# A first layer by seven products: second products added in the accumulator, and one more pair's sums moved

## The chip, the cores and the metric

The kernel runs on one core of a Trainium2 chip. A core has five engines with queues of their own: TensorE (PE; its weight loads are shown as PEld), VectorE (DVE), ScalarE (ACT), GpSimd (POOL) and SyncE (SP), which here only starts transfers. TensorE writes its products into eight accumulator banks of 128 x 512 fp32 values; ScalarE and VectorE read them there. Engines wait for each other through semaphores, and each runs its own instructions in the order in which they were written. The metric is the device time of one execution in microseconds, as the median of several runs.

## The reference

One transformer block with adaptive layer norms on 2048 rows of 512 values: a linear attention block with 32 heads, then a dense layer of 1792 columns with Mish and a dense layer back. The change lies in the second half:

```python
def _B_ref(x, w1, b1, w2):
    h = jnp.einsum("bsd,df->bsf", x, w1) + b1
    sp = jnp.log1p(jnp.exp(-jnp.abs(h))) + jnp.where(h > 0, h, jnp.zeros_like(h))
    act = h * jnp.tanh(sp)
    return jnp.einsum("bsf,fd->bsd", act, w2)

x = x + ga * _A_ref(h, A_wqkv, A_wo)
h = _layernorm(x, axis=-1) * (1 + cb) + sb
x = x + gb * _B_ref(h, B_w1, B_b1, B_w2)
```

## The kernel before

Every product of two fp32 matrices is made from three TensorE products of rounded halves: each operand is split into a high part (a ScalarE copy) and a low part (a VectorE subtraction), and hi*hi, hi*lo and lo*hi are summed in one bank (`mm3`, lines 65 to 69; `split`, 71 to 81).

The rows are worked on in four blocks of 512. The two dense layers take the blocks two at a time, with a scheme of seven products in place of eight (Strassen's, in Winograd's form) for a 2 x 2 arrangement. In the first layer the arrangement is two blocks by one *pair* g of 128-column groups of w1 (f = 2g and 2g + 1, seven pairs). `pair_unit` makes one pair's four results, each 128 x 512, from products named after their left operand:

- c11 = a11*b11 + a12*b21
- u2 = a11*b11 + s2*t2; u3 = u2 + s3*t3
- c12 = u2 + s1*t1 + s4*b22; c22 = u3 + s1*t1; the fourth is u3 + a22*t4

One `product` is six 512-column matmuls into one bank. `add` (917) is a VectorE addition of a bank and an SBUF tile. u1 is the ScalarE copy of a11*b11 out of its bank. Results go through ScalarE's Mish: `mish` (884) also splits the result at once, for the block that goes on first; `mish_b` (906) only keeps it (`ub`), for the other block.

Banks come in three kinds (`PBUFS`, 36): four "acc", three "h", one "tp". A product asks for one of a kind, and gets one that is free, or will be.

The order of work is written out by hand. Side work (splits, sums of w1's rows in `rows`, scaling and splitting w2 in `w2_job`, the layer norm of later tiles in `norm_tile`) are generators: `spawn` enters one, and each `tick` moves all of them on by one step, which puts its instructions behind those written before on their engines. An engine waits at its first unready instruction.

The stages from 200 us on: (1) the a11 and a12 products of pairs 0 and 1, between the last products of the attention output (`o_unit`); (2) for blocks 0 and 1, seven passes of `pair_unit`, each followed by the second layer of block 0 for the pair before (`trail`, `d_unit`, into the four "acc" banks `oacc`); (3) the second layer of block 1 (`second`); (4) for blocks 2 and 3 (the last block pair, L = 2), seven passes over `pairs = [5, 6, 0, 1, 2, 3, 4]`, with the second layer's first two of seven sums, m1 and m2 (`e_unit` for the pass before, four half-width "acc" banks, 24 matmuls of 256 columns, first met in pass n = 1); (5) the tail: the second layer's other sums m4, m6, m7, m5, m3, seven units each.

The tail needs *left sums* of the kept results: `left_sums` makes for one pair a split and four VectorE sums, `left_trail` runs it beside the passes of stage 4 for the first four pairs, and in the tail `ahead_of` (1145) holds what is left to prepare, one item per unit, a few units ahead of its use: the left sums of the last three pairs, then the splits for m6, m7, m5 and m3.

In the profile's names p_a and p_s are banks of products whose left operand begins with a or s, m those of the second layer's sums, l_ the left factors' halves (l_m_5l is the low half for m6 of pair 5), and buffer numbers are left out.

Of the kernel before, what the change touches and what calls it, by code (L numbers as in the profile page):

```python
# [10 lines left out]
AF = mybir.ActivationFunctionType  # L11
# [14 lines left out]
def block_kernel(ctx: ExitStack, tc: tile.TileContext, x, wqkv, wo, w1, b1t, w2, c, wmodt, out):  # L26
    nc = tc.nc
    act, dve, pool, pe, sp = nc.scalar, nc.vector, nc.gpsimd, nc.tensor, nc.sync
# [9 lines left out]
    def sb(name, dt=F32, shape=(P, 512)):  # L38

        return big.tile(list(shape), dt, tag="T", name=name, bufs=SLOTS)  # L40

    def ps(tag, name, shape=(P, 512)):
        return psp.tile(list(shape), F32, tag=tag, name=name, bufs=PBUFS[tag])
# [6 lines left out]
    def spawn(gen):  # L50
        fresh.append(gen)

    def tick():

        running.extend(fresh)
        fresh.clear()
        for g in list(running):
            if next(g, "end") == "end":
                running.remove(g)
# [5 lines left out]
    def mm3(o, st, mv, start, stop):  # L65

        pe.matmul(o, st[0], mv[0], start=start, stop=False)  # L67
        pe.matmul(o, st[0], mv[1], start=False, stop=False)  # L68
        pe.matmul(o, st[1], mv[0], start=False, stop=stop)  # L69

    def split(name, t, keep, key, lo_engine=dve, hi_engine=act):

        hi, lo = sb(f"{name}h", F32R, t.shape), sb(f"{name}l", F32R, t.shape)
        if hi_engine is act:
            act.activation(hi, t, AF.Copy)
        else:
            hi_engine.tensor_copy(hi, t)
        if lo_engine is dve:
            yield
        lo_engine.tensor_tensor(lo, t, f32(hi), op=ALU.subtract)  # L80
        keep[key] = hi, lo
# [18 lines left out]
    c0 = sb("c0")  # L100
# [71 lines left out]
    mv, rs, nb = {}, {}, {}  # L172
# [324 lines left out]
    w2s, w2d, w2f, op_a = {}, {}, {}, {}  # L497
# [9 lines left out]
    def w2_job(f, wait=2):  # L507
        if f not in w2r:
            load_w2(f)
            for _ in range(wait):  # L510
                yield
        t = w2r[f]
        dve.tensor_tensor(t, t, bc["gb"], op=ALU.mult)
        yield
        yield from split(f"w2_{f}", t, w2s, f)
        yield
        g, n = f // 2, f % 2
        if n == 0:
            w2f[g] = drp.tile([P, 2, D], F32, name=f"w2f_{g}")
            for i in range(2):  # L520
                w2d[g, i] = drp.tile([P, 2, D], F32R, name=f"w2d_{g}_{i}")
        for i in range(2):
            pool.dma_start(w2d[g, i][:, n, :], w2s[f][i])
        if g < KEPT:
            pool.dma_start(w2f[g][:, n, :], t)
# [49 lines left out]
    def rows(g, wait):  # L575

        r = [sb(f"w1p_{g}_{i}", F32, (P, 4, P)) for i in range(2)]
        for i in range(2):
            f = 2 * g + i
            sp.dma_start(r[i], w1[:, P * f:P * (f + 1)].rearrange("(k p) f -> p k f", p=P))  # L580
        for _ in range(wait):
            yield
        a11, a12, a21, a22 = [r[i][:, 2 * k:2 * k + 2, :] for i in range(2) for k in range(2)]
        s12, s34 = [sb(f"s{n}_{g}", F32, (P, 4, P)) for n in (12, 34)]
        s1, s2, s3, s4 = s12[:, 0:2, :], s12[:, 2:4, :], s34[:, 0:2, :], s34[:, 2:4, :]
        dve.tensor_tensor(s1, a21, a22, op=ALU.add)
        dve.tensor_tensor(s2, s1, a11, op=ALU.subtract)
        dve.tensor_tensor(s3, a11, a21, op=ALU.subtract)
        dve.tensor_tensor(s4, a12, s2, op=ALU.subtract)
        yield  # L590
        keep, todo = {}, []
        op_rows[g] = keep
        for name, v, parts in (("a1", r[0], ("a11", "a12")), ("s12", s12, ("s1", "s2")), ("s34", s34, ("s3", "s4")),
                               ("a22", a22, ("a22",))):
            half = split(f"{name}_{g}", v, keep, name)
            next(half)
            todo.append((name, half, parts))
            if len(todo) == 2:
                yield
                for name, half, parts in todo:  # L600
                    run(half)
                    for i, part in enumerate(parts):
                        op_a[g, part] = [h[:, 2 * i:2 * i + 2, :] for h in keep[name]]
                todo = []
# [3 lines left out]
    def store_rows(g):  # L608
        for name, halves in op_rows.pop(g).items():
            for i, h in enumerate(halves):  # L610
                rows_d[g, name, i] = drp.tile(list(h.shape), F32, name=f"rd_{g}_{name}_{i}")
                sp.dma_start(rows_d[g, name, i], f32(h))
# [151 lines left out]
    def load_back(key, src, b, t):  # L764
        v = xt[key, b, t] = sb(f"{key}b_{b}_{t}")
        sp.dma_start(v, src.pop((b, t)))

    hf, op_b = {}, {}
# [89 lines left out]
    for b in range(1, NB):  # L858
        for t in range(4):
            n = 4 * b + t  # L860
# [23 lines left out]
    def mish(p, b, f):  # L884
        u = ua[f] = sb(f"u_{b}_{f}")
        act.activation(u, p, AF.Mish, bias=b1c[:, f:f + 1])  # L886
        yield from split(f"a_{b}_{f}", u, ag, (b, f))
# [18 lines left out]
    def mish_b(p, f):  # L906

        u = ub[f] = sb(f"ub_{f}")
        act.activation(u, p, AF.Mish, bias=b1c[:, f:f + 1])  # L909

    def product(g, left, right, tag="h"):
        p = ps(tag, f"p_{left}_{g}")
        for c in range(2):
            mm3(p, [h[:, c, :] for h in op_a[g, left]], op_b[right, c], c == 0, c == 1)
        return p

    def add(out, p, u):
        dve.tensor_tensor(out, p, u, op=ALU.add)  # L918

    def pair_first(c0, g):  # L920

        u1, c11 = sb(f"u1_{g}"), sb(f"c11_{g}")
        act.activation(u1, product(g, "a11", "b11"), AF.Copy)
        add(c11, product(g, "a12", "b21"), u1)
        spawn(mish(c11, c0, 2 * g))
        return u1

    def pair_unit(c0, g, u1=None):

        f = 2 * g  # L930
        whole = u1 is None
        u2, u3, c12, c22 = [sb(f"{n}_{g}") for n in ("u2", "u3", "c12", "c22")]
        if whole:
            u1 = sb(f"u1_{g}")
            act.activation(u1, product(g, "a11", "b11"), AF.Copy)  # L935
        add(u2, product(g, "s2", "t2"), u1)
        add(u3, product(g, "s3", "t3", "tp"), u2)
        tick()
        p = product(g, "s1", "t1")
        add(c12, p, u2)  # L940
        add(c22, p, u3)
        mish_b(c22, f + 1)
        add(c12, product(g, "s4", "b22"), c12)
        mish_b(c12, f)
        tick()
        add(u3, product(g, "a22", "t4", "tp"), u3)
        spawn(mish(u3, c0, f + 1))
        if whole:
            add(u1, product(g, "a12", "b21"), u1)
            spawn(mish(u1, c0, f))  # L950
        tick()

    def prep_a(b, f):
# [35 lines left out]
            load_wb(6)  # L989


    begun = {}
    for g in range(2):
        begun[g] = pair_first(0, g)
        tick()
    for t in (2, 3):
        o_unit(NB - 1, t, "h")
# [2 lines left out]
    def trail(f):  # L1000
        if tiles:
            spawn(tiles.pop(0))
        d_unit(0, f, f)
        ahead(1, f)
        tick()

    for g in range(G + 1):
        if g < G:
            for f in (2 * g, 2 * g + 1) if g else ():
                spawn(w2_job(f))  # L1010
            if g == 0:
                spawn(rows(2, 3))
            pair_unit(0, g, begun.pop(g, None))
            if g < G - 2:
                store_rows(g)
            if 0 < g < G - 2:
                spawn(rows(g + 2, 2))
            if g == G - 1:
                for n in range(8):
                    load_back("n", nd, 2 + n // 4, n % 4)  # L1020
        for f in ((0,), (1,))[g] if g < 2 else (2 * g - 2, 2 * g - 1):
            trail(f)
# [2 lines left out]


    L = NB - 2
    pairs = [5, 6, 0, 1, 2, 3, 4]
    banks, rq, U = {}, {}, {}

    def load_r(n, c):
# [38 lines left out]
    left, sums_of = {}, {}  # L1070

    def left_trail(g):
        yield
        yield
        yield from left_sums(g)
# [48 lines left out]
    for n, g in enumerate(pairs):  # L1124
        if n < 5:
            if n:
                load_rows(n)
            if n:
                load_wb(pairs[n + 1])
        if n == 5:  # L1130
            load_wb(pairs[6])
            load_r(0, 0)
        if n == 6:
            for m in pairs[:5]:
                load_wt("m4", m)
        pair_unit(L, g)
        if n < 4:
            spawn(left_trail(g))
        if n:
            e_unit(n - 1)  # L1140
            tick()

    names = ["m4", "m6", "m7", "m5", "m3"]
    units = [(name, n) for name in names for n in range(G)]
    ahead_of = units[4:]
    loads = list(units)
    loads = loads[5:]
    load_r(1, 0)
# [22 lines left out]
    for t in range(4):  # L1171
        p = last[t][:, 0:D // 2]
# [38 lines left out]
```

## Time and profile before

| | us |
|---|---|
| median of 3 runs | 499.28 (499.13 to 499.49) |
| the profiled execution's own time | 499.34 |
| its span on the chip | 497.6 |

The span runs from the first to the last instruction of the program; some 1.7 us lie around it. A row of the timeline gives start, duration, engine, line, operation and tiles; several like instructions in a row are merged (x2), and in brackets stands how long the engine had been idle and what ended that. TensorE's matmuls overlap: the next one starts before one has ended, so their pace is read from start to start. The profile's busy shares, its waits and its timeline are shown where the prediction uses them.

### The profile page before, as it was taken

To read this page: it belongs to the slowest core of one execution; us is meant where nothing else is said; L and a number is where in the kernel's file an instruction comes from. 1 tells how busy PE (TensorE), PEld (TensorE's weight loads), DVE (VectorE), ACT (ScalarE), POOL (GpSimd) and SP (SyncE) were. 2 spreads that over 40 slices of the span, in tenths; PEclk is the share of its full clock that TensorE was granted. 3 is DMA by queue.
4 is the path that set the end of the run, shared out by engine and by line. 5 is a ranking of instruction groups with operands and counts; after the bars stand their busy time and mean duration, and the time that the engine had idled before them with its cause. 6 is when DMAs were issued, how large, how long until landed. Compare 5 with 4: busy or idle time off the path is not lost.

```text
span 497.6 us, 7730 instructions
## 1 busy us (share of the span) xinstructions
PE 490.2 (98%) x2648; PEld 412.9 (83%) x2648; DVE 394.6 (79%) x758; ACT 265.2 (53%) x472; POOL 136.8 (27%) x238
## 2 busy tenths in 40 slices
PE   7999999999999999999999999999999999999997
PEld 6778888878778888888888888888888888899997
DVE  6889775889997979986977786689878777489771
ACT  6776674533351979727677775187244444366300
POOL 3471000100212323100343333324564221544200
PEclk9999999999999999999999999999999999999999
DMA  8821413381454307298899686999998263878312
GB/s 298 295 84 44 157 33 107 129 275 43 142 139 129 96 30 251 92 366 270 239 344 312 227 278 201 335 321 383 377 343 221 66 173 86 218 189 243 91 43 86
DMA packets 65614, 96.49 MB, mean 194 GB/s; under 512 B 7277, under 2 KB 31733, under 8 KB 65574
## 3 DMA queue, kind: packets, MB, share of 16 engines
q1 hardware_dynamic: 37220, 52.51, 31.7%
q0 software_dynamic: 28208, 43.21, 30.7%
q8 instruction: 21, 0.34, 0.3%
q10 hardware_dynamic: 146, 0.26, 0.2%
q14 instruction: 19, 0.16, 0.1%
HBM read 62.92 MB, written 33.03 MB: 193 GB/s over the span
## 4 chain that ended last, share of the span: by engine, by line
PE 79%; issue 11%; POOL 4%; DVE 3%; DMA 1%; ACT 1%; POOLq 0%; DVEq 0%; ACTq 0%
PE oacc L69 5%; PE oacc L68 5%; PE oacc L67 5%; PE p_s L69 3%; PE p_s L68 3%; PE p_s L67 3%; PE o L67 3%; PE pq L67 3%; PE o L69 3%; PE o L68 3%; PE pq L69 3%; PE pq L68 3%; PE m L69 3%; PE m L68 3%; PE m L67 3%
## 5 line engine op out<-in xcount | busy, mean ns | idle before, releaser
L909 ACT ACTIVATE ub<-c,b1c 128x512 f32<-128x512 f32 x28 | 19.5, 720 | 57.3 <-DVE c L918 45.3
L918 DVE TENSOR_TENSOR u<-p_s,u 128x512 f32<-128x512 f32 x28 | 19.4, 692 | 22.8 <-PE p_s L69 12.0
L189 POOL TENSOR_TENSOR rs_n<-rs_n,half 128x1 f32<-128x1 f32 x16 | 9.8, 613 | 52.2 <-DVE rs_n L215 42.4
L918 DVE TENSOR_TENSOR u<-p_a,u 128x512 f32<-128x512 f32 x26 | 17.4, 687 | 8.3 <-PE p_a L69 8.3
L918 DVE TENSOR_TENSOR c<-p_s,u 128x512 f32<-128x512 f32 x28 | 18.0, 684 | 4.6 <-PE p_s L69 4.6
L1122 POOL DMA_DIRECT2D wt_m<-w2t x20 | 14.0, 702 | 23.3 <-PE p_s L69 15.1
L775 ACT ACTIVATE hf_n<-tp_n,mc 128x512 f32<-128x512 f32 x16 | 11.7, 772 | 16.2 <-PE tp_n L773 16.2
L886 ACT ACTIVATE u<-u,b1c 128x512 f32<-128x512 f32 x26 | 18.6, 715 | 2.8 <-DVE u L918 2.5
L241 ACT ACTIVATE e_q<-pq 128x512 f32<-128x512 f32 x16 | 9.4, 588 | 19.9 <-PE pq L69 19.9
L241 ACT ACTIVATE e_k<-pk 128x512 f32<-128x512 f32 x16 | 9.3, 590 | 13.2 <-PE pk L69 12.9
L189 POOL TENSOR_TENSOR rs_x<-rs_x,half 128x1 f32<-128x1 f32 (+1 forms) x10 | 7.1, 717 | 32.8 <-DVE rs_x L184 32.0
L573 POOL DMA_DIRECT2D w2b<-w2d x20 | 10.7, 538 | 18.4 <-DMA out_dram<-r 5.3
L243 DVE TENSOR_SCALAR e_k<-e_k 128x512 f32<-128x512 f32 x16 | 6.8, 426 | 10.1 <-ACT e_k L241 9.9
L681 POOL DMA_DIRECT2D rden_d<-rden x3 | 2.2, 740 | 43.8 <-DVE rden L679 43.8
L198 ACT ACTIVATE x<-x,nb_x,rs_x 128x512 f32<-128x512 f32 x15 | 11.6, 808 | 4.6 <-DVE nb_x L193 3.5
L567 POOL DMA_DIRECT2D wb<-w2d x14 | 9.9, 710 | 13.1 <-PE p_a L69 9.6
L935 ACT ACTIVATE u<-p_a 128x512 f32<-128x512 f32 x12 | 7.1, 588 | 10.8 <-PE p_a L69 10.1
L693 DVE TENSOR_TENSOR q<-q,rd 128x512 f32<-128x512 f32 x16 | 10.5, 686 | 2.3 <-DMA rd<-rden_d 2.2
L198 ACT ACTIVATE r<-r,nb_n,rs_n 128x512 f32<-128x512 f32 x8 | 6.5, 809 | 10.1 <-DVE nb_n L219 9.2
L705 DVE TENSOR_TENSOR r<-o,r 128x512 f32<-128x512 f32 x16 | 10.8, 683 | 1.2 <-PE o L69 1.1
L244 DVE SCALAR_TENSOR_TENSOR ku<-pk,e_k 128x512 f32<-128x512 f32 x16 | 11.1, 692 | 0.7
L244 DVE SCALAR_TENSOR_TENSOR q<-pq,e_q 128x512 f32<-128x512 f32 x16 | 11.1, 692 | 0.7
(1351 smaller groups left out, 1928.0 us busy)
## 6 DMA issues: line engine op xcount, KB each, us to landing
wm<-in_wmodt_dram SPq DMA_DIRECT2D x24, 256.0 KB, 4.8
w2b<-w2d POOLq DMA_DIRECT2D x20, 256.0 KB, 6.2
wt_m<-w2t POOLq DMA_DIRECT2D x20, 256.0 KB, 3.9
r<-in_x_dram SPq DMA_DIRECT2D x16, 256.0 KB, 2.7
x<-in_x_dram SPq DMA_DIRECT2D x15, 256.0 KB, 4.8
w1p<-in_w_dram SPq DMA_DIRECT2D x14, 256.0 KB, 5.1
w2r<-in_w_dram SPq DMA_DIRECT2D x14, 256.0 KB, 2.7
wb<-w2d POOLq DMA_DIRECT2D x14, 256.0 KB, 5.5
```

The lines of the kernel that those rows point to most:

```text
L67: pe.matmul(o, st[0], mv[0], start=start, stop=False)
L68: pe.matmul(o, st[0], mv[1], start=False, stop=False)
L69: pe.matmul(o, st[1], mv[0], start=False, stop=stop)
L189: pool.tensor_tensor(y, y, half[:, lo:hi], op=ALU.pow)
L198: act.activation(dst, t, AF.Identity, bias=nb[key, b][:, j:j + 1], scale=rs[key, b][:, j:j + 1])
L241: act.activation(e, p, AF.Exp)
L244: dve.scalar_tensor_tensor(dst, p, 0.0, e, op0=ALU.max, op1=ALU.add)
L775: act.activation(hf[b, j], p, AF.Identity, bias=mc[:, 12 + j:13 + j], scale=mc[:, 16 + j:17 + j])
L886: act.activation(u, p, AF.Mish, bias=b1c[:, f:f + 1])
L909: act.activation(u, p, AF.Mish, bias=b1c[:, f:f + 1])
L918: dve.tensor_tensor(out, p, u, op=ALU.add)
L1122: pool.dma_start(v, w2t[g][:, :, SUM[name], :])
```

## The change

`product` can take a bank that already holds a product (`onto`) and then adds to it. `pair_first` is cut in two: `pair_begin` makes a11*b11 and copies it to u1; the new `pair_first` adds a12*b21 onto the same bank and lets Mish read that bank, so that c11 needs no addition and no tile. In `pair_unit`, c22 is made first from s1*t1; then a22*t4 and c11 follow; then s4*b22 is added onto s1*t1's bank, and a single addition with u2 makes c12. a11's bank is of kind "tp" (of kind "h" for pairs 0 and 1 of the first pass, "acc" for pass n = 1 of the last blocks), and s3 and a22 move from "tp" to "h". Pairs 0 and 1 of the first pass make both a11 products before both a12. `EARLY = 5` runs the left sums of five pairs, not four, beside the passes, and the tail's list begins one item later.

```diff
--- before.py
+++ after.py
@@ -908,46 +908,48 @@
         u = ub[f] = sb(f"ub_{f}")
         act.activation(u, p, AF.Mish, bias=b1c[:, f:f + 1])
 
-    def product(g, left, right, tag="h"):
-        p = ps(tag, f"p_{left}_{g}")
+    def product(g, left, right, tag="h", onto=None):
+
+        p = onto if onto is not None else ps(tag, f"p_{left}_{g}")
         for c in range(2):
-            mm3(p, [h[:, c, :] for h in op_a[g, left]], op_b[right, c], c == 0, c == 1)
+            a, b = [h[:, c, :] for h in op_a[g, left]], op_b[right, c]
+            for i, (st, mv) in enumerate(((a[0], b[0]), (a[0], b[1]), (a[1], b[0]))):
+                pe.matmul(p, st, mv, start=onto is None and c == 0 and i == 0, stop=c == 1 and i == 2,
+                          skip_group_check=onto is not None)
         return p
 
     def add(out, p, u):
         dve.tensor_tensor(out, p, u, op=ALU.add)
 
-    def pair_first(c0, g):
-
-        u1, c11 = sb(f"u1_{g}"), sb(f"c11_{g}")
-        act.activation(u1, product(g, "a11", "b11"), AF.Copy)
-        add(c11, product(g, "a12", "b21"), u1)
-        spawn(mish(c11, c0, 2 * g))
-        return u1
-
-    def pair_unit(c0, g, u1=None):
+    def pair_begin(g, tag):
+
+        u1, p = sb(f"u1_{g}"), product(g, "a11", "b11", tag)
+        act.activation(u1, p, AF.Copy)
+        return u1, p
+
+    def pair_first(c0, g, p):
+        spawn(mish(product(g, "a12", "b21", onto=p), c0, 2 * g))
+
+    def pair_unit(c0, g, u1=None, tag="tp"):
 
         f = 2 * g
-        whole = u1 is None
         u2, u3, c12, c22 = [sb(f"{n}_{g}") for n in ("u2", "u3", "c12", "c22")]
-        if whole:
-            u1 = sb(f"u1_{g}")
-            act.activation(u1, product(g, "a11", "b11"), AF.Copy)
+        p11 = None
+        if u1 is None:
+            u1, p11 = pair_begin(g, tag)
         add(u2, product(g, "s2", "t2"), u1)
-        add(u3, product(g, "s3", "t3", "tp"), u2)
+        add(u3, product(g, "s3", "t3"), u2)
         tick()
         p = product(g, "s1", "t1")
-        add(c12, p, u2)
         add(c22, p, u3)
         mish_b(c22, f + 1)
-        add(c12, product(g, "s4", "b22"), c12)
+        add(u3, product(g, "a22", "t4"), u3)
+        spawn(mish(u3, c0, f + 1))
+        tick()
+        if p11 is not None:
+            pair_first(c0, g, p11)
+        add(c12, product(g, "s4", "b22", onto=p), u2)
         mish_b(c12, f)
-        tick()
-        add(u3, product(g, "a22", "t4", "tp"), u3)
-        spawn(mish(u3, c0, f + 1))
-        if whole:
-            add(u1, product(g, "a12", "b21"), u1)
-            spawn(mish(u1, c0, f))
         tick()
 
     def prep_a(b, f):
@@ -989,9 +991,10 @@
             load_wb(6)
 
 
-    begun = {}
+    begun = [pair_begin(g, "h") for g in range(2)]
+    tick()
     for g in range(2):
-        begun[g] = pair_first(0, g)
+        pair_first(0, g, begun[g][1])
         tick()
     for t in (2, 3):
         o_unit(NB - 1, t, "h")
@@ -1010,7 +1013,7 @@
                 spawn(w2_job(f))
             if g == 0:
                 spawn(rows(2, 3))
-            pair_unit(0, g, begun.pop(g, None))
+            pair_unit(0, g, begun[g][0] if g < 2 else None)
             if g < G - 2:
                 store_rows(g)
             if 0 < g < G - 2:
@@ -1025,7 +1028,7 @@
 
 
     L = NB - 2
-    pairs = [5, 6, 0, 1, 2, 3, 4]
+    pairs, EARLY = [5, 6, 0, 1, 2, 3, 4], 5
     banks, rq, U = {}, {}, {}
 
     def load_r(n, c):
@@ -1133,8 +1136,8 @@
         if n == 6:
             for m in pairs[:5]:
                 load_wt("m4", m)
-        pair_unit(L, g)
-        if n < 4:
+        pair_unit(L, g, tag="acc" if n == 1 else "tp")
+        if n < EARLY:
             spawn(left_trail(g))
         if n:
             e_unit(n - 1)
@@ -1142,7 +1145,7 @@
 
     names = ["m4", "m6", "m7", "m5", "m3"]
     units = [(name, n) for name in names for n in range(G)]
-    ahead_of = units[4:]
+    ahead_of = units[EARLY:]
     loads = list(units)
     loads = loads[5:]
     load_r(1, 0)
```

## The prediction, made before the result was known

> **What bounds the kernel now.** I read the page's first two parts, then TensorE's waits and its busy time by stage, then the timeline at the only longer wait. Columns of the windows: stretch, its length, busy time (instructions) of PE, the granted clock, DMA share, GB/s; where more engines stand: PE, PEld, DVE, ACT, POOL.
>
> ```profile
> span 497.6 us, 7730 instructions
> ...
> PE 490.2 (98%) x2648; PEld 412.9 (83%) x2648; DVE 394.6 (79%) x758; ACT 265.2 (53%) x472; POOL 136.8 (27%) x238
> ```
>
> ```profile
> PE m L69 <- DVE l_m_5l L80: 0.6, 1, 0.6
> ```
>
> ```profile
> 204.00:356.00 152.00, 152.00 (x686) 1.00 0.89 293
> 356.00:440.00 84.00, 84.00 (x441) 1.00 0.74 200
> 440.00:454.00 14.00, 13.36 (x112) 1.00 0.77 201
> 454.00:494.00 40.00, 40.00 (x334) 1.00 0.35 98
> ```
>
> ```profile
> 452.83 0.28 PE L67 MATMUL m<-wt_m,l_m_5h 128*128 128x256 f32 x1
> 452.95 0.28 PE L68 MATMUL m<-wt_m,l_m_5h 128*128 128x256 f32 x1
> 453.87 0.39 PE L69 MATMUL m<-wt_m,l_m_5l 128*128 128x256 f32 x1 [0.64 <-DVE l_m_5l L80]
> ...
> 455.16 0.28 PE L67 MATMUL m<-wt_m,l_m_6h 128*128 128x256 f32 x1
> ```
>
> From 204 us on, where every changed line lies, TensorE is never idle but once: at 453, when m6 begins and the low half of its first left factor is late. Two 256-column matmuls start 0.12 us apart (452.83, 452.95). A group of twelve should take 1.44 us; this one took 455.16 - 452.83 = 2.33. The wait costs 0.89 us: 0.80 of lateness (453.87 against 453.07) and 0.09 of restarting. No matmul is added or removed, so a faster kernel can come only from such gaps: -0.89 us is practically the most there is, and any new wait of TensorE is paid in full.
>
> **The additions.** Each of the 14 pair passes had seven VectorE additions and will have five; c12's first addition and c11's go.
>
> ```profile
> L918 DVE TENSOR_TENSOR c<-p_s,c 128x512 f32<-128x512 f32 x14 | 9.6, 687 | 0.5
> L909 ACT ACTIVATE ub<-c,b1c 128x512 f32<-128x512 f32 x28 | 19.5, 720 | 57.3 <-DVE c L918 45.3
> L775 ACT ACTIVATE hf_n<-tp_n,mc 128x512 f32<-128x512 f32 x16 | 11.7, 772 | 16.2 <-PE tp_n L773 16.2
> ```
>
> 28 x 0.687 = 19 us of VectorE work vanish, but under a TensorE that is busy 152.00 of 152.00 and 84.00 of 84.00 us they are worth nothing where they go. The price is in the banks: a12 can be added onto a11's bank only after the copy to u1; s4 onto s1's only after c22's addition has read it; and a11's bank stays taken until ScalarE's Mish has read it. Mish of a bank isn't in the trace; nearest are Mish of SBUF (0.72) and the affine pass from a bank (0.77). I take 0.72, with 0.59 (a plain copy, below) and 0.77 as ends. The accumulating matmuls themselves I cost at nothing: five of six in each product accumulate already.
>
> **One pair's sums moved.** With EARLY = 5 the five VectorE operations of the fifth pair's left sums leave the tail for the seventh pair's pass.
>
> ```profile
> 439.95 0.68 DVE L80 TENSOR_TENSOR l_2l<-ub,l_2h 128x512 fp32r<-128x512 f32 x1
> 443.46 0.68 DVE L80 TENSOR_TENSOR l_3l<-ub,l_3h 128x512 fp32r<-128x512 f32 x1
> 453.13 0.68 DVE L80 TENSOR_TENSOR l_m_5l<-u,l_m_5h 128x512 fp32r<-128x512 f32 x1
> ```
>
> ```profile
> 427.45:439.87 12.42, 12.42 (x69) 10.76 (x67) 6.13 (x10) 5.29 (x9) 6.99 (x10) 1.00 0.92 234
> ```
>
> They fill 439.95 to 443.46: 3.51 us. Ahead of that, VectorE has 12.42 - 6.13 = 6.3 us free in the seventh pass, and two additions fewer. So l_m_5l comes near 449.6 against a need at 453.07; even pushed back 1 us by earlier waits it has over 2 us in hand. The 0.89 us go. What would be late next, the remaining left factors, each stand a unit earlier than before too. One ScalarE copy moves with them, into a pass with 7.1 us free there. SP's and POOL's queues hold the same transfers in the same order as before. Term: **-0.89**.
>
> **New waits, pass by pass.** Pairs and passes count as in the code, pairs from 0. The new order in a pass is a11, s2, s3, s1, a22, a12, s4, so s4 stands where a12 stood.
>
> Start of the first layer: a11 of pairs 0 and 1 run one after the other, then both a12.
>
> ```profile
> 205.15 0.60 ACT L923 ACTIVATE u<-p_a 128x512 f32<-128x512 f32 x1 [1.79 <-PE p_a L69]
> ```
>
> A product's six matmuls take 1.36 us (286.55 - 283.83 below is two of them). The copy follows the last matmul of a11 by 0.43 (the lag found below), so that one started at 204.72 and, past the other a11, a12 is due at 204.72 + 0.23 + 1.36 = 206.31; the copy ends at 205.75. The second is 1.36 us behind: 207.11 against 207.67. Hidden by the other pair's product; if ScalarE were over 0.56 us later, the wait would show one for one.
>
> Pairs 3 to 5 of the first pass are near the edge, since ScalarE copies u1 late there and VectorE has the next rows' sums between u3 and c.
>
> ```profile
> 257.19 1.34 ACT L909 ACTIVATE ub<-c,b1c 128x512 f32<-128x512 f32 x2 [0.44 <-DVE c L918]
> 272.44 1.34 ACT L909 ACTIVATE ub<-c,b1c 128x512 f32<-128x512 f32 x2 [0.44 <-DVE c L918]
> 282.79 0.58 ACT L935 ACTIVATE u<-p_a 128x512 f32<-128x512 f32 x1
> ```
>
> ```profile
> 255.88 1.28 DVE L918 TENSOR_TENSOR c<-p_s,u 128x512 f32<-128x512 f32 x2
> 271.13 1.28 DVE L918 TENSOR_TENSOR c<-p_s,u 128x512 f32<-128x512 f32 x2
> 283.39 1.49 DVE L918 TENSOR_TENSOR u<-p_s,u 128x512 f32<-128x512 f32 x2 [1.79 <-ACT u L935]
> 286.39 1.28 DVE L918 TENSOR_TENSOR c<-p_s,u 128x512 f32<-128x512 f32 x2
> ```
>
> ```profile
> 256.63 0.39 PE L67 MATMUL p_a<-b_2h,a_3h 128*128 128x512 f32 x1
> 271.59 0.39 PE L67 MATMUL p_a<-b_2h,a_4h 128*128 128x512 f32 x1
> 283.83 0.39 PE L67 MATMUL p_s<-b_2h,s_5h 128*128 128x512 f32 x1
> 286.55 0.39 PE L67 MATMUL p_a<-b_2h,a_5h 128*128 128x512 f32 x1
> ```
>
> c22 now stands in c12's place and lasts 0.69 us. Pair 3: 255.88 + 0.69 = 256.57, s4 due at 256.63: just hidden. Pair 4 with the old start: 271.82 + 0.06 against 271.59, 0.29 us late. Pair 5: a22 now takes s2's bank, due at 283.83, while u2's addition would read it until 284.08. But the copies that start these chains come earlier: ScalarE's Mish of c22 waited 0.44 us for c22 to follow c12, and c22 is now first, so from pair 3 to 4 and again from 4 to 5 the chain gains 0.44. With 0.44, c22 of pair 4 ends at 271.38, and with 0.88 u2 of pair 5 ends at 283.20 and c22 at 286.20, all in time. Term: **0**; without that gain 0.29 + 0.31 + 0.17 with 0.09 of restart each, about 1.0.
>
> Last block, first pass:
>
> ```profile
> 363.41 1.28 DVE L918 TENSOR_TENSOR c<-p_s,u 128x512 f32<-128x512 f32 x2
> 364.02 0.39 PE L67 MATMUL p_a<-b_0h,a_5h 128*128 128x512 f32 x1
> ```
>
> c22 ends at 364.10, seen by TensorE 0.06 later (453.13 + 0.68 to 453.87): 0.14 late, and 0.09 of restart. Term: **+0.23**.
>
> Second pass: its a11 takes a bank of the "acc" tag, which in the built program is the one that m2's second half gets.
>
> ```profile
> 374.16 1.34 ACT L909 ACTIVATE ub<-c,b1c 128x512 f32<-128x512 f32 x2 [3.95 <-DVE c L918]
> 375.40 0.62 ACT L75 ACTIVATE l_5h<-ub 128x512 fp32r<-128x512 f32 x1
> 375.93 0.71 ACT L886 ACTIVATE u<-u,b1c 128x512 f32<-128x512 f32 x1
> ```
>
> ```profile
> 374.67 0.39 PE L69 MATMUL p_a<-b_1h,a_6l 128*128 128x512 f32 x1
> 377.05 0.28 PE L67 MATMUL m<-wb,a_11h 128*128 128x256 f32 x1
> ```
>
> ```profile
> 399.51 0.39 PE L69 MATMUL p_a<-b_1h,a1b 128*128 128x512 f32 x1
> 402.61 0.40 PE L67 MATMUL p_a<-b_0h,a1b 128*128 128x512 f32 x1
> ```
>
> ```profile
> 399.94 0.69 DVE L918 TENSOR_TENSOR u<-p_a,u 128x512 f32<-128x512 f32 x1 [0.67 <-PE p_a L69]
> ```
>
> An addition follows the last matmul's start by 0.43 (399.51, 399.94). So c12: 375.10 to 375.79; Mish of c12 at 375.84; behind it in ScalarE's order l_5h at +0.62, then Mish of c11 at +0.53, 376.99 to 377.71, seen at 377.77. m2's second half is due at 377.05: 0.72 late, 0.09 restart. Behind that matmul TensorE's whole queue stands. Term: **+0.81**; ends 0.68 (0.59 for the Mish) and 0.86. Nothing excludes zero if the bank were another, which is rival 1.
>
> Passes 3 to 7 give the bank to the next pass's a11, with no l_h between the two Mishes: from 399.51, c12 until 400.63, Mishes from 400.68 and 401.30 until 402.02, due at 402.61: 0.53 in hand. Term 0.
>
> The sum is -0.89 + 0.23 + 0.81 = +0.15 on the profiled execution's 499.34, which stands 0.06 above the median 499.28: **499.4 us**.
>
> **A rule against it.** The 0.64 us gap at 453 lies in a stretch whose granted clock reads 1.00. The Trainium skill, "TensorE: Matmul & The Clock Gate", section "A second HAM failure mode: psum-queue depth-cycling", says that small idles between groups which cycle through banks can make the clock fall back and rise again. By the row the new waits cost only themselves; by that rule a pass could run at a lower clock, rival 4.
>
> **Rivals.**
> 1. Gain only: the wait at m2 doesn't show (another bank, or c11's Mish in time). 499.28 - 0.89 + (0 to 0.23) = 498.4 to 498.6. For it: an "acc" bank was chosen for this one pass. Against: the order c12, l_5h, c11 in ScalarE.
> 2. Slower: in pairs 4 and 5 the copies of u1 start no earlier than 267.5 and 282.79. Then the 1.0 worked out above comes on top: 500.4. For it: Mish of c12 now comes later in ScalarE's order and could open new idles; against: its work from pass to pass is the same and 0.44 of it was waiting.
> 3. Slower: passes 3 to 6 of the last block lose their 0.53 because something else stands ahead of the Mishes; were it two copies (0.53 each, as l_5h), each of the four passes would lose 0.53 and 0.09 of restart: 499.4 + 2.5 = 501.9. Against: in the order as built only c12's Mish stands there.
> 4. The clock drops for a pass: at half rate its 12.42 us double, 511.9. Against: 1.00 in all four stretches.
> 5. Over 1 us faster, were VectorE's relief also to remove small gaps that the waits don't list: 498.2.
>
> **How the numbers follow.** Forecast 0.55 (own range 499.0 to 499.9), rivals 1 to 5: 0.15, 0.18, 0.05, 0.02, 0.05. A change under 0.2% (1.0 us) can't be told from none: the line is at 498.28 and 500.28. The forecast and rival 1 lie within; so 0.70 the same, 0.25 slower (2, 3, 4), 0.05 faster. Leaving out 3, 4 and 5 and no more, the range reaches from rival 1's 498.4 to 500.5.
>
> **What would show it.** Right: no wait of TensorE on l_m_5l; one of about 0.7 us at the seventh matmul of m2's first unit, released by a Mish; one of about 0.1 at s4 of the last block's first pass, released by VectorE; additions on VectorE 28 fewer; none in pairs 3 to 5. Wrong: waits of a22 or s4 there, or a wait of a11 on a Mish from the third pass on; a clock below 1.00; or TensorE's 0.227 us step changed in the accumulating products.

## The result, and the profile after

| | before | changed |
|---|---|---|
| median (us) | 499.38 (499.12 to 499.69, 18 runs) | 500.27 (500.07 to 500.81, 18 runs) |
| profiled execution (us) | 499.34 | 500.48 |
| its span (us) | 497.6 | 498.8 |

The ratio of the two is 1.0018, with a 95% interval of 1.0011 to 1.0026. So the changed kernel is slower by 0.6 to 1.3 us. The forecast was 499.4.

The page of the changed kernel, span and busy times:

```profile
span 498.8 us, 7659 instructions
...
PE 491.2 (98%) x2648; PEld 412.7 (83%) x2648; DVE 378.1 (76%) x730; ACT 264.5 (53%) x472; POOL 137.3 (28%) x238
```

VectorE has 28 instructions fewer (730 against 758) and 16.5 us less to do (378.1 against 394.6), and the end did not come earlier.

TensorE's busy time by stage in the changed kernel, columns as in the prediction (stretch, length, then PE, PEld, DVE, ACT and POOL, then granted clock, DMA share and GB/s):

```profile
204.00:356.00 152.00, 151.86 (x684) 124.97 (x683) 115.22 (x219) 92.88 (x174) 46.76 (x86) 1.00 0.88 289
356.00:440.00 84.00, 83.52 (x428) 71.25 (x427) 54.73 (x87) 34.44 (x56) 32.50 (x54) 1.00 0.73 198
440.00:454.00 14.00, 14.00 (x119) 14.00 (x118) 12.12 (x19) 11.01 (x21) 5.12 (x8) 1.00 0.80 192
454.00:494.00 40.00, 40.00 (x336) 40.00 (x335) 26.65 (x45) 7.80 (x15) 7.27 (x14) 1.00 0.43 117
```

The gap of the stage from 440 us on has gone; the first two stages, full before, have gaps now. Busy time understates them, because a matmul that waits only a little starts before the one ahead has ended. So TensorE is read from start to start: 0.227 us between 512-column matmuls, 0.120 between 256-column ones, and what exceeds that was lost. TensorE's timeline in the changed kernel shows the three places where it lost time that it does not lose in before, and m6's start, where it loses none any more:

```profile
254.02 0.39 PE L917 MATMUL p_s<-t_1h,s_3l 128*128 128x512 f32 x1
254.55 0.50 PE L917 MATMUL p_a<-t_0h,a_3h 128*128 128x512 f32 x1
254.89 0.40 PE L917 MATMUL p_a<-t_0l,a_3h 128*128 128x512 f32 x1
...
257.21 0.39 PE L917 MATMUL p_a<-b_3h,a_3l 128*128 128x512 f32 x1
257.52 0.50 PE L917 MATMUL p_s<-b_2h,s_3h 128*128 128x512 f32 x1
...
364.81 0.39 PE L917 MATMUL p_a<-b_1h,a_5l 128*128 128x512 f32 x1
365.18 0.50 PE L917 MATMUL p_s<-b_0h,s_5h 128*128 128x512 f32 x1
...
378.22 0.28 PE L69 MATMUL m<-wb,a_11l 128*128 128x256 f32 x1
378.98 0.39 PE L67 MATMUL m<-wb,a_11h 128*128 128x256 f32 x1 [0.48 <-ACT u L886]
...
454.98 0.28 PE L68 MATMUL m<-wt_m,l_m_5h 128*128 128x256 f32 x1
455.10 0.28 PE L69 MATMUL m<-wt_m,l_m_5l 128*128 128x256 f32 x1
```

| place | predicted | measured |
|---|---|---|
| m6's l_m_5l | -0.89 | -0.91 (in before 0.80 and 0.10 of restart) |
| m2's second half, pass n = 1 | +0.81 | +0.75 (0.64 + 0.10) |
| s4, first pass of the last block | +0.23 | +0.24 (0.13 + 0.11) |
| a22 and s4 of pair 3, first layer | 0 | +0.62 (0.30 + 0.13, 0.08 + 0.11) |
| pairs 4 and 5; last passes 3 to 7 | 0 | 0 |
| sum | +0.15 | +0.70 |

For instance m2: 378.98 - 378.22 - 0.12 = 0.64; the second number in brackets is the restart, by which the matmuls just behind a wait start late too. The profiled executions lie 1.14 us apart. Of this 0.33 was there before any changed line ran: one and the same product of the attention output starts at 200.74 in before and at 201.07 here. That is a difference between two executions, not of the change. The 0.1 us that are left after 0.70 + 0.33 is spread in pieces too small to place. The medians, 0.89 apart, agree with 0.70 within their interval.

### The profile page after: what moved, and what is told of

Same layout as the page of the kernel before. It is cut to its first block, busy times and chain, and to the rows that moved or that the text cites. A ratio compares the mean times of both kernels' runs of the same rounds, so it can differ in the third digit from the quotient of the medians.

```text
span 498.8 us, 7659 instructions
## 1 busy us (share of the span) xinstructions
PE 491.2 (98%) x2648; PEld 412.7 (83%) x2648; DVE 378.1 (76%) x730; ACT 264.5 (53%) x472; POOL 137.3 (28%) x238
## 4 chain that ended last, share of the span: by engine, by line
PE 93%; DVE 3%; ACT 2%; DMA 1%; issue 1%; POOL 0%; ACTq 0%
PE p_s L917 15%; PE p_a L917 11%; PE oacc L69 5%; PE oacc L67 5%; PE oacc L68 5%; PE m L67 5%; PE m L69 5%; PE m L68 5%; PE o L67 3%; PE pq L67 3%; PE o L69 3%; PE o L68 3%; PE pq L69 3%; PE pq L68 3%; PE gacc L68 3%; PE gacc L69 3%
## 5 line engine op out<-in xcount | busy, mean ns | idle before, releaser
L922 DVE TENSOR_TENSOR c<-p_s,u 128x512 f32<-128x512 f32 x28 | 19.3, 689 | 24.1 <-PE p_s L917 24.0
L927 ACT ACTIVATE u<-p_a 128x512 f32<-128x512 f32 x14 | 8.3, 591 | 13.6 <-PE p_a L917 12.1
L198 ACT ACTIVATE x<-x,nb_x,rs_x 128x512 f32<-128x512 f32 x15 | 11.6, 807 | 4.6 <-DVE nb_x L193 3.5
L922 DVE TENSOR_TENSOR u<-p_a,u 128x512 f32<-128x512 f32 x14 | 9.7, 692 | 5.7 <-PE p_a L917 5.0
L198 ACT ACTIVATE r<-r,nb_n,rs_n 128x512 f32<-128x512 f32 x8 | 6.5, 812 | 12.0 <-DVE nb_n L219 9.2
L886 ACT ACTIVATE u<-u,b1c 128x512 f32<-128x512 f32 x14 | 10.0, 715 | 2.6 <-DVE u L922 2.2
```

Of the source, the lines that this page charges most:

```text
L198: act.activation(dst, t, AF.Identity, bias=nb[key, b][:, j:j + 1], scale=rs[key, b][:, j:j + 1])
```

## Where pair 3's waits come from

ScalarE's timeline, first in the kernel before, then in the changed one:

```profile
240.98 1.34 ACT L909 ACTIVATE ub<-c,b1c 128x512 f32<-128x512 f32 x2 [4.04 <-DVE c L918]
243.16 0.82 ACT L198 ACTIVATE r<-r,nb_n,rs_n 128x512 f32<-128x512 f32 x1 [0.84 <-ACT ub L909]
...
252.27 0.58 ACT L935 ACTIVATE u<-p_a 128x512 f32<-128x512 f32 x1
```

```profile
241.13 0.72 ACT L909 ACTIVATE ub<-c,b1c 128x512 f32<-128x512 f32 x1 [3.42 <-DVE c L922]
243.51 0.82 ACT L198 ACTIVATE r<-r,nb_n,rs_n 128x512 f32<-128x512 f32 x1 [1.65 <-DMA w2d<-w_2h]
...
245.51 0.71 ACT L909 ACTIVATE ub<-c,b1c 128x512 f32<-128x512 f32 x1
...
253.19 0.58 ACT L927 ACTIVATE u<-p_a 128x512 f32<-128x512 f32 x1
```

In pass 2 ScalarE comes to a layer norm step (L198) that isn't ready yet. It reads nb_n, which VectorE makes (L219) from 242.92 to 243.07 in before and from 243.27 to 243.42 here; the brackets of L198 name other releasers, but in both kernels it starts 0.09 us after nb_n's end. The 0.35 us between the two is the distance of the two executions, so this wait has not moved. Before, both Mishes (c22's and c12's) ran ahead of it, in time in which ScalarE would have been idle. Now c12 is finished later, so only c22's stands ahead (x1, not x2); ScalarE idles 1.65 us instead of 0.84, and c12's Mish runs at 245.51, behind the step. From L198 to pair 3's copy of u1 there are now 253.19 - 243.51 = 9.68 us of work, where there were 252.27 - 243.16 = 9.11: 0.57 more, about the time that one more Mish occupies. VectorE's timeline in the changed kernel shows what follows:

```profile
253.80 1.47 DVE L922 TENSOR_TENSOR u<-p_s,u 128x512 f32<-128x512 f32 x2 [1.79 <-ACT u L927]
255.19 0.41 DVE L586 TENSOR_TENSOR s<-w1p 128x256 f32<-128x256 f32 x1
...
256.79 0.68 DVE L922 TENSOR_TENSOR c<-p_s,u 128x512 f32<-128x512 f32 x1
```

u2's addition starts when the copy ends and reads s2's bank until about 254.49; a22 wants that bank at 254.25 and starts at 254.55. c22's addition, behind the sums of w1's rows (L586), reads s1's bank until 257.47; s4 wanted it at 257.44, and starts at 257.52.

## The experiments

Each was timed in turn with the kernel before, whose median was 499.4 to 499.5 in all of them. Diffs are against the changed kernel unless said otherwise.

**1. The moved sums alone, on either side.** First the changed kernel without that part:

```diff
-    pairs, EARLY = [5, 6, 0, 1, 2, 3, 4], 5
+    pairs, EARLY = [5, 6, 0, 1, 2, 3, 4], 4
```

> The changed kernel with EARLY = 4: the fifth pair's left sums stay in the tail. Theory A (TensorE is always busy, so each of its waits counts in full and nothing else counts): the wait on m6's first left factor returns and costs about 0.9 us, so 501.1 us (before is 499.4, the changed kernel 500.3). Rival R1 (the 28 additions that VectorE no longer makes bring that factor in time by themselves, and EARLY = 5 gains nothing): 500.3 us and no wait on m6.

501.70 us (501.67 to 501.77, 5 runs), ratio 1.0046 [1.0034, 1.0059]: 0.6 above the expected 501.1. VectorE's and TensorE's timelines in that kernel:

```profile
441.77 0.69 DVE L80 TENSOR_TENSOR a_8l<-u,a_8h 128x512 fp32r<-128x512 f32 x1 [1.43 <-ACT a_8h L75]
442.38 0.68 DVE L80 TENSOR_TENSOR l_2l<-ub,l_2h 128x512 fp32r<-128x512 f32 x1
```

```profile
454.81 0.28 PE L68 MATMUL m<-wt_m,l_m_5h 128*128 128x256 f32 x1
456.29 0.39 PE L69 MATMUL m<-wt_m,l_m_5l 128*128 128x256 f32 x1 [1.21 <-DVE l_m_5l L80]
```

The wait comes back, and larger: 456.29 - 454.81 - 0.12 = 1.36 us against 0.80 in before. In the accumulating form c11's Mish stands last in a pass, behind c12's, so its low half (a_8l) comes late in VectorE's queue, right ahead of the tail's left sums: VectorE idles 1.43 us for it, and the left sums begin at 442.38, where before has 439.95, 2.43 us later. TensorE is 1.86 later there (the matmul at 454.81 ran at 452.95 in before). The 0.57 between them is what the wait grew by, and what the expectation, which had counted the old wait alone, fell short by.

Then the kernel before, with that part alone (diff against before):

```diff
-        if n < 4:
+        if n < 5:
             spawn(left_trail(g))
...
-    ahead_of = units[4:]
+    ahead_of = units[5:]
```

> The kernel before with nothing changed but five pairs' left sums beside the passes, not four. Theory A: the wait of 0.89 us on m6's left factor goes and none comes: 498.5 us. Rival R1: the wait stays, 499.4 us; or the five operations make VectorE late in the seventh pass and a wait shows there.

498.54 us (498.30 to 498.98, 11 runs), ratio 0.9983 [0.9974, 0.9992]; the wait at m6 is gone and no other has come. So the moved sums are worth 499.40 - 498.54 = 0.86 us on their own, and the accumulating form on its own costs 501.70 - 499.40 = 2.3 us. Beside the moved sums it costs 500.27 - 498.54 = 1.7, because they also cover what it adds to the wait at m6.

**2. c11 ahead of a22**, so that c11's Mish would no longer stand behind c12's:

```diff
+        if p11 is not None:
+            pair_first(c0, g, p11)
         add(u3, product(g, "a22", "t4"), u3)
         spawn(mish(u3, c0, f + 1))
         tick()
-        if p11 is not None:
-            pair_first(c0, g, p11)
         add(c12, product(g, "s4", "b22", onto=p), u2)
```

> The changed kernel with a12 (onto a11's bank) ahead of a22 in each pass, so that a22 asks 1.36 us later for the bank that u2's addition reads, and Mish of c11 stands ahead of Mish of c12 and of the left sums' copy on ScalarE. Theory A: the waits of a22 in pair 3 (0.43 us) and of m2's second half (0.75) go, those of s4 in pair 3 (0.19) and in the last block's first pass (0.24) stay: 499.1 us. Rival R2 (what the changed kernel lost lies in accumulating onto a bank that was read, not in the two waits): it stays at 500.0 us or above.

500.46 us (500.34 to 500.64, 11 runs), ratio 1.0021 [1.0012, 1.0030]: a miss. The waits of m2 and of a22 went, as expected, but others took their place. TensorE's timeline and ScalarE's in that kernel:

```profile
248.31 0.39 PE L69 MATMUL oacc<-w_3h,a_3l 128*128 128x512 f32 x1
248.76 0.50 PE L917 MATMUL p_a<-b_0h,a_3h 128*128 128x512 f32 x1
...
257.19 0.39 PE L917 MATMUL p_a<-t_1h,a_3l 128*128 128x512 f32 x1
258.26 0.50 PE L917 MATMUL p_s<-b_2h,s_3h 128*128 128x512 f32 x1 [0.69 <-DVE c L922]
```

```profile
244.25 0.82 ACT L198 ACTIVATE r<-r,nb_n,rs_n 128x512 f32<-128x512 f32 x1 [2.67 <-DVE nb_n L219]
...
248.10 0.61 ACT L75 ACTIVATE a_3h<-w1p 128x512 fp32r<-128x512 f32 x1
...
253.94 0.58 ACT L927 ACTIVATE u<-p_a 128x512 f32<-128x512 f32 x1
```

The layer norm step is ready later (244.25, against 243.51 in the changed kernel), since nb_n stands in VectorE's queue behind an addition that now waits for a22; and c11's Mish and its split stand ahead of the copy of w1's next row group. So that copy (a_3h) runs at 248.10 where the changed kernel has 246.12, and pair 3's a11 waits for it (0.23 at 248.31, and 0.39 more behind it with the restarts). u1's copy is later still, and s4 waits 0.85 for c22. ScalarE's queue can be reordered, but something must stand last in it. The time is also what the rival had named, that accumulating onto a bank that was read costs something by itself. This run alone doesn't exclude that, though its timeline puts the time into waits for these instructions; experiments 6 and 7, in which the accumulating form loses nothing, leave that rival no room.

**3. The same, and the first tick behind c22**, so that the side work that this tick puts into VectorE's queue (sums of w1's rows in pair 3, splits and sums of w2's rows in the last block's first pass) no longer stands ahead of c22's addition:

```diff
-        tick()
         p = product(g, "s1", "t1")
...
         mish_b(c22, f + 1)
+        tick()
+        if p11 is not None:
+            pair_first(c0, g, p11)
...
         tick()
-        if p11 is not None:
-            pair_first(c0, g, p11)
```

> As the run with a12 ahead of a22, and the first tick of a pass stands behind c22's addition, so that no side work stands between u3 and c22 on VectorE. Theory A: the two waits of s4 go too, no wait of TensorE is left after 204 us beyond those around 350 us that the kernel before has too: 498.6 us, the same as the kernel before with EARLY = 5 alone. Rival R3 (the side work that is now later makes its readers late): a new wait, 499.1 us or above.

499.22 us (499.08 to 499.58, 11 runs), ratio 0.9996 [0.9987, 1.0005]. Every wait of s4 is gone, in the last block too; the tick's place is all that differs from experiment 2. a11's wait in pair 3 stays (248.31 and 248.76 are again the starts), 0.68 us in all with its restarts and one small wait behind; that is about the distance from the 498.6 expected. The rival's time, 499.1 or above, came true, but not for its reason: the wait that is left was there in experiment 2, and the later side work adds none.

**4. One more copy on ScalarE**, to test the chains themselves. A copy of c22 onto itself, in pass 2 of the first blocks and in pass n = 1 of the last, right behind c12's Mish:

```diff
         mish_b(c12, f)
+        if (c0, g) in ((0, 2), (NB - 2, 6)):
+            act.activation(c22, c22, AF.Copy)
```

> The changed kernel with one needless 128x512 ScalarE copy behind Mish of c12 in pass 2 of the first layer's first stage and in pass 1 of the last block. Theory A (both waits are set by ScalarE's order: what stands between Mish of c12 and the late instruction counts one for one): m2's wait grows from 0.64 by the 0.53 us of a copy, and a22's wait on u2 in pair 3 from 0.30 by 0.53; 501.3 us. Rival R2 (a fixed cost of accumulating onto, or taking over, a bank): both waits stay, 500.3 us.

501.41 us (501.22 to 501.46, 4 runs), ratio 1.0038 [1.0024, 1.0052]. TensorE's timeline in that kernel:

```profile
253.93 0.39 PE L917 MATMUL p_s<-t_1h,s_3l 128*128 128x512 f32 x1
254.97 0.50 PE L917 MATMUL p_a<-t_0h,a_3h 128*128 128x512 f32 x1 [0.66 <-DVE u L922]
...
378.64 0.28 PE L69 MATMUL m<-wb,a_11l 128*128 128x256 f32 x1
379.92 0.38 PE L67 MATMUL m<-wb,a_11h 128*128 128x256 f32 x1 [1.00 <-ACT u L886]
```

a22's wait grew from 0.30 to 0.82 and m2's from 0.64 to 1.16: 0.52 each, one copy's step in ScalarE's queue, one for one. Both waits end at ScalarE's queue and have nothing in hand.

**5. u1 copied by VectorE** in passes 2 to 6 of the first blocks, with everything else as changed:

```diff
-    def pair_begin(g, tag):
+    def pair_begin(g, tag, on_dve=False):
...
-        act.activation(u1, p, AF.Copy)
+        if on_dve:
+            dve.tensor_copy(u1, p)
+        else:
+            act.activation(u1, p, AF.Copy)
...
-            u1, p11 = pair_begin(g, tag)
+            u1, p11 = pair_begin(g, tag, c0 == 0)
```

> The changed kernel with u1 copied by VectorE in the first stage's passes 2 to 6. Theory A (pair 3's waits of a22 and s4, 0.62 us with their restarts, come from ScalarE copying u1 late): they go, those of the last block (0.24 and 0.75) stay; 499.7 us. Rival R4 (VectorE itself is late there, by its side work): they stay, 500.3 us or above.

499.59 us (499.31 to 500.35, 11 runs), ratio 1.0005 [0.9996, 1.0014]. VectorE's timeline in that kernel:

```profile
252.16 1.47 DVE L922 TENSOR_TENSOR u<-p_s,u 128x512 f32<-128x512 f32 x2
```

u2's addition starts at 252.16 instead of 253.80, and pair 3's waits are gone; the last block's two stay (0.13 and 0.64, with restarts). So the copy's place in ScalarE's queue is what both of pair 3's waits need; for s4, moving the tick was enough too (experiment 3).

**6. All waits out**: experiment 5, with experiment 3's tick, and c11 ahead of a22 in the last block alone (diff against experiment 5).

```diff
-        tick()
         p = product(g, "s1", "t1")
...
         mish_b(c22, f + 1)
+        tick()
+        if p11 is not None and c0:
+            pair_first(c0, g, p11)
         add(u3, product(g, "a22", "t4"), u3)
         spawn(mish(u3, c0, f + 1))
         tick()
-        if p11 is not None:
+        if p11 is not None and not c0:
             pair_first(c0, g, p11)
```

> All three repairs together: u1 copied by VectorE in the first stage, a12 ahead of a22 in the last block only, the first tick of a pass behind c22. Theory A: no wait of TensorE after 204 us but those around 350 us; 498.5 us, equal to the kernel before with EARLY = 5, that is 28 additions fewer are worth nothing. Rival R5 (the relief of VectorE is worth something once the waits are out): below 498.3 us.

498.54 us (498.29 to 500.10, 11 runs), ratio 0.9984 [0.9976, 0.9993]: the same as the kernel before with the moved sums alone, which still has its 28 additions. Its profiled execution took 499.25 and has one long wait, besides small ones around 350 us that before has too. VectorE's and TensorE's timelines there:

```profile
327.94 0.42 DVE L545 TENSOR_TENSOR t<-w2p,t 128x256 f32<-128x256 f32 x1 [0.82 <-DMA w2p<-w2f]
...
347.78 0.69 DVE L80 TENSOR_TENSOR a_7l<-ub,a_7h 128x512 fp32r<-128x512 f32 x1
```

```profile
347.42 0.39 PE L68 MATMUL oacc<-w2b,a_7h 128*128 128x512 f32 x1
348.52 0.50 PE L69 MATMUL oacc<-w2b,a_7l 128*128 128x512 f32 x1 [0.71 <-DVE a_7l L80]
```

In that execution VectorE waited 0.8 us for a load of w2's rows, as it does at this place in no other profile of this study. Its queue is full from there on, and twenty microseconds later TensorE waits 0.87 for the low half a_7l (348.52 - 347.42 - 0.23).

**7. Those low halves a unit earlier**, once on the kernel before with the moved sums alone, once on experiment 6. Both prepare block 1's kept results earlier by the same edit, although the second expectation speaks of the last block:

```diff
-        if 0 <= u - NF + 3 < NF:
-            spawn(prep_a(b, last_first[u - NF + 3]))
+        if 0 <= u - NF + 4 < NF:
+            spawn(prep_a(b, last_first[u - NF + 4]))
```

> The kernel before with EARLY = 5, and in the second layer of block 1 each left factor's split entered one step earlier (four units ahead instead of three). Theory A: the waits on low halves around 350 us (0.36 us in all before) go, 498.2 us. Rival: VectorE's queue is full there, and another low half is late: 498.5 us or above.

> The kernel of e11_all_waits_out, and the rows of the last block's first sums (a_h, a_l of the prepared features) entered four units ahead instead of three, as in e12_before_five_prep_earlier. Theory A (all of the time above 498.15 is waits of TensorE; the 28 additions fewer are worth nothing): 498.15, equal to e12_before_five_prep_earlier within 0.2%, ratio about 0.9975, no wait of TensorE after 204 us. Rival R6 (VectorE's queue around 336 us is late in the accumulating form for a reason of its own, which is what a_7l waited for in e11_all_waits_out's profiled execution): entering the rows a unit earlier does not help, a wait on a_7l or a_8l near 347 to 350 stays and the median is 498.5 or more. Rival R7 (additions off VectorE's queue are worth something once the waits are out): 497.5 or less.

498.15 us (497.92 to 498.24, 7 runs), ratio 0.9973 [0.9961, 0.9984], and 498.21 us (497.77 to 498.37, 8 runs), ratio 0.9973 [0.9962, 0.9984]. TensorE's stretches in the first, then in the second:

```profile
204.00:356.00 152.00, 152.00 (x688) 126.24 (x687) 124.36 (x236) 94.38 (x175) 45.52 (x84) 1.00 0.88 291
356.00:440.00 84.00, 84.00 (x441) 72.49 (x440) 63.58 (x100) 36.73 (x58) 34.22 (x58) 1.00 0.75 202
```

```profile
204.00:356.00 152.00, 152.00 (x688) 126.19 (x687) 119.78 (x226) 91.80 (x170) 45.42 (x84) 1.00 0.89 292
356.00:440.00 84.00, 84.00 (x442) 72.50 (x441) 55.65 (x87) 36.81 (x58) 34.07 (x57) 1.00 0.76 202
```

TensorE is busy all through in both, start to start at its pace (0.09 us behind each group of transposes left aside, which every kernel here has), and the times are equal, though VectorE has 12.5 us less to do in these stretches in the second (187.94 against 175.43). These two are the fastest kernels of the study, 0.27% under before. The 0.39 us that the first gains on 498.54 is about the 0.36 that before loses around 350 us. It needs four edited lines; the accumulating form adds nothing to it.

## Why the prediction was right and where it was not

*The bound.* Right in kind. No matmul was added or removed, the differences that can be placed are gaps of TensorE, and 28 additions fewer are worth nothing (experiments 6 and 7, against the same kernels with the additions). The additions weighed less than the 19 us counted: VectorE's busy time fell by 16.5, and two additions in a row last 1.28 us, not 2 x 0.687. And TensorE was idle more than "but once". The prediction read that from busy time (152.00 of 152.00) and from the list of waits, which both leave out waits as short as these. TensorE's timeline in before:

```profile
350.36 0.39 PE L68 MATMUL oacc<-w2b,a_8h 128*128 128x512 f32 x1
350.73 0.50 PE L69 MATMUL oacc<-w2b,a_8l 128*128 128x512 f32 x1
351.07 0.39 PE L67 MATMUL oacc<-w2b,a_8h 128*128 128x512 f32 x1
```

These starts are 0.37 and 0.34 us apart instead of 0.227, and one at 347.72 is 0.33 ahead of the next: 0.36 us in all, and the changed kernel loses 0.34 there too. So 0.89 was not the most that there is to gain; experiment 7 took this too. Rival 5 had reckoned with small gaps, but VectorE's relief did not remove them.

*The moved sums, -0.89.* Right at 0.91. VectorE's timeline in the changed kernel:

```profile
442.56 0.68 DVE L80 TENSOR_TENSOR l_3l<-ub,l_3h 128x512 fp32r<-128x512 f32 x1
452.23 0.68 DVE L80 TENSOR_TENSOR l_m_5l<-u,l_m_5h 128x512 fp32r<-128x512 f32 x1
```

The gain came with less in hand than it looks: l_m_5l runs at 452.23, not near 449.6, since the tail's left sums begin at 442.56, 2.6 us later than in before (the queue of experiment 1). It ends at 452.91 and is used at 455.10, so 2.2 us were in hand. By the prediction's own figures it would have been 453.07 - 449.6 - 0.68 = 2.8; its "over 2 us" with 1 us of push-back left out the 0.68 that the subtraction lasts, so the likeness of the two numbers is luck. The 0.6 less is what experiment 1 shows. What the prediction didn't see is that the accumulating form by itself makes this wait larger; the moved sums cover 1.47 us there, not 0.91.

*The last block, +0.23 and +0.81.* Right in place, releaser and nearly in size. ScalarE's timeline of the changed kernel has the order that was foreseen, and gives the one term that was off:

```profile
377.12 0.72 ACT L909 ACTIVATE ub<-c,b1c 128x512 f32<-128x512 f32 x1 [1.33 <-DVE c L922]
377.75 0.61 ACT L75 ACTIVATE l_5h<-ub 128x512 fp32r<-128x512 f32 x1
378.27 0.67 ACT L886 ACTIVATE u<-p_a,b1c 128x512 f32<-128x512 f32 x1
```

Mish of a bank lasts 0.67, where 0.72 was taken (between ends of 0.59 and 0.77). That is 0.05 of the 0.06 by which the term was too large.

*Pairs 3 to 5, "Term: 0".* This step failed, for pair 3. The prediction put the new sequence onto pair 3's start in the profile of before (255.88 + 0.69 = 256.57, "just hidden") and let ScalarE's chain change only from pair 3 on, and only for the better. But pass 2 is a changed pass too. Its second Mish moved behind a layer norm step that ScalarE waits for anyway, so idle time that had held a Mish was lost, and the copy of u1 came 0.57 late. For a22, whose bank it checked for pair 5, it gave no figure here. VectorE's timeline in before has one:

```profile
252.88 1.49 DVE L918 TENSOR_TENSOR u<-p_s,u 128x512 f32<-128x512 f32 x2 [1.79 <-ACT u L935]
```

u2's addition would leave s2's bank at 252.88 + 0.69 = 253.57, and a22 would want it two products ahead of s4, at 256.63 - 2.72 = 253.91: 0.34 us in hand, and 0.57 was lost. The 0.23 between them and the 0.06 until TensorE sees it are the wait of 0.30.

Rival 2 named this mechanism ("Mish of c12 now comes later in ScalarE's order and could open new idles"), but priced it for pairs 4 and 5, where there was none, and put against it that the work from pass to pass is the same. The work is; its place against a fixed wait is not. Experiments 4 and 5 show the chain from ScalarE's queue to the wait; that the place of c12's Mish is what filled the queue is read from the timelines, and no run puts that Mish back. This step alone takes the sum from +0.15 to about +0.7. The price of 1.0 in rival 2 stays untested: it takes each wait from the times of before, although a wait of TensorE in pair 4 would have given pair 5 more time.

*The clock.* The granted clock is 1.00 in all four stretches of the changed kernel, waits of 0.13 to 0.64 included, and in experiment 1 beside a wait of 1.36. The rule of the Trainium skill, "TensorE: Matmul & The Clock Gate", section "A second HAM failure mode: psum-queue depth-cycling", that frequent small idles between groups of matmuls can throttle the clock, did not come into play here: a handful of waits is not the every-iteration cycling that it describes.

*The verdict.* The largest chance went to no change within 0.2%. The median is 0.18% slower and the interval reaches from 0.11% to 0.26%, so it lies at the very edge of that: that 500.27 falls on this side of the line at 500.28 is luck. The time is inside the range from 498.4 to 500.5, but outside the forecast's own 499.0 to 499.9, and 0.87 us above the forecast. Of the signs that the prediction named, those of being right came, except that pair 3 waits; waits of a22 and s4 there were its first sign of being wrong.

## What to carry to other kernels

When an order is changed in every pass, follow an engine's queue from the pass before the one in question: a step that leaves the time ahead of a wait which stays where it is loses idle time that was free, even where the sum of work stays the same. An accumulation in place of an addition saves work on the adding engine, but it makes the second product wait for all readers of the first one's bank; count that where the matmul engine is the bound. Read a pipelined engine from start to start, since its busy time hid 0.36 us of waits here. And separate the parts of a change: here one part gave 0.86 us, the other took more, and the part that gave was the better kernel alone.

## What the runs showed of the hardware

- Behind each of TensorE's waits in the table of the result and in experiments 1 and 4, of 0.08 or of 1.36 us alike, another 0.10 to 0.13 us was lost, because the matmuls behind it start late too (254.55 to 254.89 is 0.34 instead of 0.227).
- Matmuls that add onto a bank filled by an earlier product keep the pace of 0.227 us. The only price of accumulating that these runs show is in waits: with all of them out, the times are equal with and without it (498.21 and 498.15).
- ScalarE's Mish is shorter from a bank (0.67 us) than from SBUF (0.72); an activation in its queue counts less than its own duration: the added copy lasts 0.62 and delayed the chain by 0.52.
- VectorE once waited 0.8 us for a load, and TensorE waited 0.87 us twenty microseconds later, since the VectorE queue between was full; that execution took 0.7 us more than the median (499.25, 498.54). Whether the same lies behind that kernel's slowest run (500.10) was not seen.
